# Experts 2 to 8 in the order of their load, with rooms cut to rank and a folded last tile

## The chip, the cores and the metric

The kernel runs on one core of one Trainium2 chip. The metric is the device time in microseconds (us) from one launch: the median over the runs that are shown. Engines are named as the profile names them: PE (TensorE, matrix products), PEld (its weight loads), DVE (VectorE), ACT (ScalarE), POOL (GpSimd) and SP (SyncE, which here only starts transfers).

## The reference

Attention of 4 batches, 8 heads, 576 positions and 64 per head, once over means of four positions and once over a band of |i - j| < 4, is added up to rows `x` (2304 x 512). Each row then goes to the 2 of 8 experts with the highest noisy gate value:

```python
logits = x @ w_gate
noisy_logits = logits + np.log1p(np.exp(x @ w_noise)) * noise
top2 = np.argpartition(-noisy_logits, 2, axis=1)[:, :2]
# top2_w: softmax over the two values
for e in range(E):
    for k in range(2):
        mask = top2[:, k] == e
        h = np.maximum(x[mask] @ w1[e], 0.0)            # 512 x 1024
        out[mask] += top2_w[mask, k, None] * (h @ w2[e])  # 1024 x 512
```

Everything is float32. For the reference's own inputs the eight experts get 619, 579, 568, 539, 545, 556, 609 and 593 rows.

## The kernel before

**Number format.** Products of the experts run in the type fp32r, each operand split in a high part (the operand rounded by a copy to fp32r) and a low part (what is left). A product is three: high x high, low x high, high x low.

**Early part (up to 232 us).** Attention, gating, the lists of rows per expert, and all of expert 0. Its work is written as steps (`Step`), each with an engine, a planned duration, buffers and a priority. `run_steps` plans: of the steps that can run it takes the one that starts first, priority breaking ties, and emits the instructions in that order. The priority is that of the step's place plus an offset by kind from the table `OFF` (L322). Stages 1 to 3 of this plan follow one another. For each row the two list entries (row number and weight) are scattered into `list_d` in DRAM (`r_put`); expert e's list begins at `e * LST`. After the last group of rows `c_count` adds up the counts and `c_tiles` works out how many tiles of 128 rows stand beyond each expert's room, `CAP` = 630 slots.

**Experts 1 to 7.** This part is written out in program order, in a loop over the experts. `NT` = 5 tiles of `TR` = 126 rows are an expert's room; 632 columns in two halves of 316 are multiplied. For expert e:

- `gemm1(e, f)`, f = 0 to 7: PE multiplies 128 columns of w1 (the weights in the array) with the 2 x 316 columns of `xh`, `xl` (2 halves x 4 chunks x 3 products = 24 products). ACT takes the relu out of PSUM into `hh`, DVE the rest into `hl`. PSUM has two buffers for this.
- `gemm2(e, t)`, t = 0 to 4: 126 rows of `hh`, `hl` are the weights in the array and w2 streams 512 columns (8 chunks x 3 products = 24). DVE scales by the row's weight and adds what stands in `out` (fetched by `load_acc`); POOL scatters the sum to `out`.

Beside these, by the table `BESIDE` (slots 0 to 7 are the groups of `gemm1`, 8 to 12 the tiles of `gemm2`), the next expert's rows are brought: `gather` (G, POOL), `turn_xt` (T, a 32 x 32 transpose on DVE), `move_xt` (M, N; copies of 32 partitions, half on ACT, half on DVE) and `make_xt` (H, the split in high and low). The order of tile 4 is G4 in slot 9, T4 in 10, M4 and N4 in 11, H4 in 12. SP fetches w2 in the course of `gemm1` and the next expert's w1 in the course of `gemm2`, through three buffers `raw`; ACT and DVE split them (`split_hi`, `split_lo`). At the start of an expert SP loads the next one's list (`load_list`) and DVE limits its row numbers (`list_rows`).

**Beyond the room.** At the end all engines read whether any expert has more rows than its room; if so, a block loads that expert's weights (w1 and w2, 4.19 MB) anew and works through further tiles of 128 rows with nothing beside it.

Of the kernel before, what the change touches and what calls it, by code (L numbers as in the profile page):

```python
# [22 lines left out]
def kernel(  # L23
# [12 lines left out]
    nc = tc.nc  # L36
# [33 lines left out]
    LST = P * ((CAP + P * ((N - CAP + P - 1) // P) + P - 1) // P)  # L70
    FAR = 4096
    PST = 4
# [39 lines left out]
    counts = cpool.tile([P, E], F32, tag="counts", name="counts")  # L112
    cnt16 = cpool.tile([P, E], BF16, tag="cnt16", name="cnt16")
# [20 lines left out]
    def c_route():  # L134
# [9 lines left out]
                       allow_small_or_imprecise_dtypes=True)  # L144
        nc.gpsimd.iota(base_e, pattern=[[LST, E]], base=0, channel_multiplier=0,
# [40 lines left out]
    raws = {}  # L186

    def fetch_w(e, z, f):
        if z == 0:
            raw = stage.tile([P, NDC, P], F32, tag="raw", name="raw1")  # L190
            nc.sync.dma_start(out=raw, in_=w1[e, :, f * P : (f + 1) * P].rearrange("(c p) f -> p c f", p=P))
# [82 lines left out]
    def run_steps(stage):  # L274
# [48 lines left out]
        "a_acc": -44.2, "a_count": -60, "a_holes": 6, "a_list": 10.6, "a_part": -60, "a_rows": 25.3,  # L323
        "b_gather": -60, "b_gemm": 30.3, "b_hi": 10.9, "b_list": -11.9, "b_lo": -21.5, "b_order": -10.6,
        "b_pe": -23.8, "b_relu": -27.6, "b_rest": -44.4, "b_rows": 35.1, "b_weights": -26.1, "c_count": -49,
        "c_fills": 39, "c_first": -42.1, "c_ids": -17.6, "c_masks": -48.5, "c_route": -37.4, "c_sel": -58.3,
        "c_tiles": -59, "d_exp": -3.6, "d_max": -23.4, "d_norm": 16.4, "d_pt": -8.8, "d_ptc": -15.8,
        "d_pv": -48.8, "d_qk": -27.5, "d_rz": 44.4, "d_up": -8.5, "e_go": 43.4, "e_hi": -60, "e_lo": 46.5,
        "e_order": -58.5, "e_pe": -2.9, "fetch_e": 11.3, "fetch_w1": 31.8, "fetch_w2": 20.9,
        "fill_list": -37.6, "fill_out": 41.4, "gather": 18.4, "hi_e": 51.9, "identb": 30, "init_kz": 60,  # L330
        "l_exp": -60, "l_lg": -27.3, "l_lgc": 27.8, "l_lgt": -15.1, "l_load_v": 26.2, "l_ls": -19.8,
        "l_max": 23.1, "l_norm": -10.7, "l_pt": 7.2, "l_ptc": 21.8, "l_pv": 10.8, "l_qk": 1.7,
        "l_store": -24.5, "l_sum": 50.9, "l_x": -58.2, "l_xt": -20.9, "l_xtc": 26.7, "list_rows": 3.3,
        "lo_e": -50.5, "load_list": 59.2, "load_noise": 30.4, "load_wgn": -14.6, "masks": 17, "o_mul": -60,
        "o_part": -15, "o_put": 41.7, "ones": 2.2, "r_count": 52.3, "r_hot": -5.6, "r_oh": -20.5, "r_pay": -29,
        "r_pos": -35.2, "r_put": 17.7, "r_slot": 37, "r_soft": -59.5, "r_top": -52.3, "r_wexp": 53.9,
        "r_where": -60, "split_hi1": 28.3, "split_hi2": -26.7, "split_lo1": 60, "split_lo2": 29.4,
        "t_copy": -52.9, "t_load": -18, "t_new": 16.1, "t_pe": 11.6, "t_sum": 14.9, "t_sumq": -28.2,
        "vd_load": -1.6, "vd_sum": 2.8, "vd_sum2": 26.4, "warm": 30.2}
# [759 lines left out]
    def load_list(e):  # L1099

        src = list_d[e * LST : e * LST + NT * P, :]
        lt = l_p.tile([P, NT, 2], I32, tag="lt", name=f"lt{e}")
        wait_for(nc.sync.dma_start(out=lt, in_=src.rearrange("(p t) c -> p t c", t=NT)), scatters)
        lists[e] = lt, None

    def list_rows(e):
        lt = lists[e][0]
        cl = l_p.tile([P, NT], I32, tag="cl", name=f"cl{e}")
        nc.vector.tensor_scalar_min(cl, lt[:, :, 0], N - 1)
        lists[e] = lt, cl  # L1110
# [9 lines left out]
    def gather(e, t):  # L1120
        gx = gx_p.tile([P, DM], F32, tag="gx", name=f"gx{e}_{t}")
        ins = nc.gpsimd.indirect_dma_start(  # L1122
            out=gx, out_offset=None, in_=x_rows[:, :],
            in_offset=bass.IndirectOffsetOnAxis(ap=lists[e][1][:, t : t + 1], axis=0))
# [3 lines left out]
    def new_xt(e):  # L1128
        xeT[e] = (xe_p[e % 2].tile([P, NDC, NCOL], F32R, tag="xh", name=f"xh{e}"),
                  xe_p[e % 2].tile([P, NDC, NCOL], F32R, tag="xl", name=f"xl{e}"))  # L1130
# [58 lines left out]

# [3 lines left out]

    def c_tiles():
        nc.vector.tensor_copy(cnt_f[:, 0:E], st.pop("pc"))
        nc.vector.tensor_tensor(cnt_f[:, 0:1], cnt_f[:, 0:1], base_e[:, 0:1], op=ALU.add)
        nc.vector.tensor_reduce(out=cnt_f[:, E:], in_=cnt_f[:, 0:E], axis=AX.X, op=ALU.max)
        nc.vector.tensor_scalar(cnt_f, cnt_f, float(P - 1 - CAP), 0.0, op0=ALU.add, op1=ALU.max)
# [5 lines left out]
    def turn_xt(e, t):  # L1204
        tr = gx_p.tile([P, 4, NDC, 32], F32, tag="tr", name=f"tr{e}_{t}", bufs=2)
        nc.vector.transpose(out=tr, in_=gxs.pop((e, t)).rearrange("p (a c j) -> p a c j", a=4, c=NDC))
        trs[e, t] = tr

    def move_xt(e, t, us):
# [3 lines left out]
        for u in us:  # L1213
            for a in range(4):
# [5 lines left out]

    def make_xt(e, t):
# [3 lines left out]
        sl = slice(t * TR, t * TR + P)  # L1225
        xr = xrs.pop((e, t)).rearrange("p u (c i) -> p c u i", c=NDC)
        xh, xl = (x_[:, :, sl].rearrange("p c (u i) -> p c u i", u=4) for x_ in xeT[e])
# [6 lines left out]
    def o_part(t, c):  # L1234
# [4 lines left out]
        for f in range(OC * c, OC * (c + 1)):  # L1239
            hh, hl = hts[f]  # L1240
# [21 lines left out]
    def e_hi(t):  # L1262
        if t == 0:
            new_xt(1)
        sl, src = cols(t)
        nc.scalar.activation(xeT[1][0][:, :, sl], st["ptg", t][:, :, src], AF.Copy)

    def e_lo(t):
        sl, src = cols(t)
        nc.vector.tensor_tensor(xeT[1][1][:, :, sl], st.pop(("ptg", t))[:, :, src], xeT[1][0][:, :, sl].bitcast(F32), op=ALU.subtract)  # L1270
# [5 lines left out]

    def gemm1(e, f):
        xh, xl = xeT[e]
        wh, wl = w1s[f]
        ph = ps_h.tile([P, 2, 512], F32, tag="sc", name=f"ph{e}_{f}")  # L1280
        for n in range(2):
            sl = slice(n * NH, (n + 1) * NH)
# [4 lines left out]
        hts[f] = (h_p.tile([P, NCOL], F32R, tag=f"hh{f}", name=f"hh{e}_{f}"), h_p.tile([P, NCOL], F32R, tag=f"hl{f}", name=f"hl{e}_{f}"))  # L1287
        hh, hl = (x.rearrange("p (n m) -> p n m", n=2) for x in hts[f])
        nc.scalar.activation(hh, ph[:, :, 0:NH], AF.Relu)  # L1289
        nc.vector.scalar_tensor_tensor(out=hl, in0=ph[:, :, 0:NH], scalar=0.0, in1=hh.bitcast(F32),  # L1290
# [226 lines left out]
```

## Time and profile before

| | |
|---|---|
| median of 3 runs | 633.02 us (632.44 to 633.78) |
| the profiled execution: its time | 634.73 us |
| its span, first to last instruction | 633.0 us |
| mean granted TensorE clock in the span | 0.981 of full |
| busy: PE, PEld, DVE, ACT, POOL | 603.8, 525.9, 398.7, 335.6, 239.7 us |
| moved between HBM and core | 72.62 MB read, 19.95 MB written |

The span is measured inside one profiled execution; its time has what lies around the span as well. A busy share is a mean over parts of the kernel with different limits. PE's matmuls overlap and their ends are modelled, so the pace of a run of products is read from the chain, as its length over their number, and not from the duration of one.

### The profile page before, as it was taken

What the parts mean: (1) busy time and instruction counts of PE and PEld (TensorE: products, weight loads), DVE (VectorE), ACT (ScalarE), POOL (GpSimd) and SP (SyncE); (2) the same over time, 40 slices, a digit from 0 to 9 for tenths busy, and PEclk for the clock granted to TensorE, in tenths of its full rate; (3) what the DMA queues carried; (4) which work ended last, traced back from release to release, by engine and by line L of the source; (5) the groups of instructions that cost most, each with busy time, mean ns of one, the idle gap of its engine ahead of it and who ended that gap; (6) DMA issues with size and microseconds to landing.
All of it is one profiled execution on the core that took longest, in us unless ns stands there. A gap on an engine that the chain in (4) does not pass through costs nothing.

```text
span 633.0 us, 12482 instructions
## 1 busy us (share of the span) xinstructions
PE 603.8 (95%) x4598; PEld 525.9 (83%) x4598; DVE 398.7 (63%) x1019; ACT 335.6 (53%) x770; POOL 239.7 (38%) x310
## 2 busy tenths in 40 slices
PE   8899997998998999999999999999999999999993
PEld 7668775767987889889988988998899899889982
DVE  5987797896865445873775587377458737754310
ACT  7967785775644224752763475266357526633200
POOL 6585457762564423323222322323232232322111
PEclk9999999898899999999999999999999999999997
DMA  9987888967545715444553545455354545444111
GB/s 193 164 169 150 210 197 165 252 189 204 155 112 140 222 44 170 132 145 152 150 154 112 165 124 152 142 153 155 116 155 129 160 143 143 150 131 123 52 47 35
DMA packets 137010, 92.61 MB, mean 146 GB/s; under 512 B 72280, under 2 KB 118872, under 8 KB 136940
## 3 DMA queue, kind: packets, MB, share of 16 engines
q1 hardware_dynamic: 125388, 62.71, 40.4%
q0 software_dynamic: 11552, 29.01, 15.0%
q8 instruction: 38, 0.62, 0.4%
q14 instruction: 32, 0.26, 0.2%
HBM read 72.62 MB, written 19.95 MB: 146 GB/s over the span
## 4 chain that ended last, share of the span: by engine, by line
PE 82%; DMA 7%; ACT 3%; POOL 3%; DVE 2%; issue 1%; SPq 1%; POOLq 0%; DVEq 0%
PE ph L1285 31%; PE py L1310 31%; PE py L1243 3%; PE o L661 3%; DMA raw<-in_moe_w_dram 2%; PE ph0b L1170 2%; PE sc L613 2%; PE pt L438 2%; DMA vw<-in_v_dram 2%; PE ptx L692 1%; PE od L576 1%; PE ptl L646 1%; DMA vg<-in_v_dram 1%; POOL list_d L869 1%; PE ptd L554 1%
## 5 line engine op out<-in xcount | busy, mean ns | idle before, releaser
L1285 PE MATMUL ph<-xl,w0h 128*128 128x316 f32 x448 | 137.9, 308 | 0.0
L1285 PE MATMUL ph<-xh,w0l 128*128 128x316 f32 x448 | 137.8, 308 | 0.0
L1285 PE MATMUL ph<-xh,w0h 128*128 128x316 f32 x448 | 137.7, 307 | 0.0
L1289 ACT ACTIVATE hh<-ph 128x632 fp32r<-128x632 f32 x56 | 39.2, 700 | 134.8 <-PE ph L1285 134.8
L1310 PE MATMUL py<-w1h,hl 128*126 128x512 f32 x280 | 110.4, 394 | 0.0
L1310 PE MATMUL py<-w1h,hh 128*126 128x512 f32 x280 | 110.3, 394 | 0.0
L1310 PE MATMUL py<-w1l,hh 128*126 128x512 f32 x280 | 110.3, 394 | 0.0
L1290 DVE SCALAR_TENSOR_TENSOR hl<-ph,hh 128x632 fp32r<-128x632 f32 x56 | 45.7, 817 | 85.0 <-ACT hh L1289 85.0
L1316 POOL DMA_INDIRECT out_dram<-ga,lt x35 | 39.2, 1120 | 155.0 <-DVE ga L1315 123.7
L1285 PEld LDWEIGHTS ph<-xh,w0h 128*128 128x128 f32 x448 | 84.3, 188 | 0.3
L1285 PEld LDWEIGHTS ph<-xl,w0h 128*128 128x128 f32 x448 | 84.3, 188 | 0.3
L1285 PEld LDWEIGHTS ph<-xh,w0l 128*128 128x128 f32 x448 | 84.2, 188 | 0.0
L1217 ACT ACTIVATE xr<-tr 32x128 f32<-32x128 f32 x240 | 74.0, 308 | 3.4
L1315 DVE SCALAR_TENSOR_TENSOR ga<-py,lt,ga 126x512 f32<-126x512 f32 x35 | 26.3, 751 | 68.2 <-PE py L1310 68.2
L1298 POOL DMA_INDIRECT ga<-out_dram,cl x35 | 37.6, 1073 | 82.8 <-PE ph L1285 61.0
L201 ACT ACTIVATE w0h<-raw 128x512 fp32r<-128x512 f32 x64 | 39.4, 625 | 48.4 <-DMA raw<-in_moe_w_dram 48.2
L1310 PEld LDWEIGHTS py<-w1l,hh 128*126 128x126 f32 x280 | 52.1, 186 | 12.9
L1310 PEld LDWEIGHTS py<-w1h,hh 128*126 128x126 f32 x280 | 52.2, 186 | 12.6
L1310 PEld LDWEIGHTS py<-w1h,hl 128*126 128x126 f32 x280 | 52.1, 186 | 12.5
L1219 DVE COPY xr<-tr 32x128 f32<-32x128 f32 x240 | 54.6, 227 | 3.0
L1122 POOL DMA_INDIRECT gx<-x_d,cl x35 | 36.7, 1048 | 51.9 <-PE ph L1285 33.4
L869 POOL DMA_INDIRECT list_d<-pay,sli x36 | 36.9, 1025 | 43.1 <-DMA x_d<-x 12.8
(196 smaller groups left out, 1080.5 us busy)
## 6 DMA issues: line engine op xcount, KB each, us to landing
raw<-in_moe_w_dram SPq DMA_DIRECT2D x128, 256.0 KB
vw<-in_v_dram SPq DMA_DIRECT2D x80, 64.0 KB
x_d<-x SPq DMA_DIRECT2D x18, 256.0 KB
out_dram<-zero SPq DMA_DIRECT2D x6, 768.0 KB
nat<-in_q_dram SPq DMA_DIRECT2D x16, 256.0 KB
nat<-in_k_dram SPq DMA_DIRECT2D x16, 256.0 KB
vg<-in_v_dram SPq DMA_DIRECT2D x8, 320.0 KB
vg<-in_v_dram SPq DMA_DIRECT2D x8, 256.0 KB
```

The costliest lines, as they stand in the source:

```text
L201: nc.scalar.activation(hi, raw, AF.Copy)
L869: ins = nc.gpsimd.indirect_dma_start(out=list_d[:, :], out_offset=bass.IndirectOffsetOnAxis(ap=sli[:, kk, i : i + 1], axis=0), in_=pay[:, ...
L1122: ins = nc.gpsimd.indirect_dma_start(out=gx, out_offset=None, in_=x_rows[:, :], in_offset=bass.IndirectOffsetOnAxis(ap=lists[e][1][:, t : ...
L1217: nc.scalar.activation(dst, src, AF.Copy)
L1219: nc.vector.tensor_copy(dst, src)
L1285: last_mm[0] = nc.tensor.matmul(ph[:, n, 0:NH], lhsT=w[:, c, :], rhs=xx[:, c, sl], start=(c == 0 and z == 0), stop=(c == NDC - 1 and z == 2))
L1289: nc.scalar.activation(hh, ph[:, :, 0:NH], AF.Relu)
L1290: nc.vector.scalar_tensor_tensor(out=hl, in0=ph[:, :, 0:NH], scalar=0.0, in1=hh.bitcast(F32), op0=ALU.max, op1=ALU.subtract)
L1298: after_pe(nc.gpsimd.indirect_dma_start(out=acc[:TR], out_offset=None, in_=out[:, :], in_offset=bass.IndirectOffsetOnAxis(ap=cl[:TR, t : t ...
L1310: last_mm[0] = nc.tensor.matmul(py[:TR], lhsT=hx[:, sl], rhs=w, start=(f == 0 and z == 0), stop=(f == NFC - 1 and z == 2))
L1315: nc.vector.scalar_tensor_tensor(out=acc[:TR], in0=py[:TR], scalar=wt, in1=acc[:TR], op0=ALU.mult, op1=ALU.add)
L1316: nc.gpsimd.indirect_dma_start(out=out[:, :], out_offset=bass.IndirectOffsetOnAxis(ap=lt[:TR, t, 0:1], axis=0), in_=acc[:TR], in_offset=No ...
```

## The change

The seven experts after expert 0 are taken in the order of their number of rows, largest first. The order is worked out on the chip (`c_rank`) and a register on SP holds each rank's expert number (`read_which`); weights and lists are fetched at addresses from that register. Rank r has a room of its own: 512 slots in four tiles of 128 rows, and a last tile of 112, 96, 80 and four times 64 slots, that is 624, 608, 592 and 4 x 576. Expert 0 stays first, with its room of 630 in tiles of 126.

`gemm1` multiplies two halves of 312, 304, 296 or 288 columns. Where the last tile has 64 slots, the columns of `x` are placed so that each half has two tiles and 32 of the tail; the relu and its rest are taken out in two pieces, and `h` is laid out so that the tail's high and low parts stand side by side. `gemm2` of this tile loads them as 128 rows against the high part of w2 (rows 0 to 63 then have high x high, rows 64 to 127 low x high) and adds high x low to rows 0 to 63: 16 products for 24. The lower rows are then copied out of PSUM by ACT and added by DVE ahead of the scaling.

Lists are loaded in two pieces; gathers, transposes and splits of the last tile work on its rows alone. In the early part there are two more steps (`c_rank` on DVE, `which` on SP), and `load_list` and `fetch_e` of expert 1 wait for the latter. Every number of the table `OFF` is another. `LST` grows from 2432 to 2560 slots.

```diff
-    LST = P * ((CAP + P * ((N - CAP + P - 1) // P) + P - 1) // P)
+    LST = P + P * ((CAP + P * ((N - CAP + P - 1) // P) + P - 1) // P)
+    MAIN = (NT - 1) * P
+    FOLD = 64
+    HALF = 2 * P + FOLD // 2
+    TAIL = [None, 112, 96, 80] + [FOLD] * (E - 4)
+    def cap(r):
+        return MAIN + TAIL[r] if r else CAP
...
+    def read_which(r):
+        which[r] = nc.values_load(perm[0:1, r : r + 1], engines=[mybir.EngineType.SP], min_val=0, max_val=E - 1,
...
-            nc.sync.dma_start(out=raw, in_=w2[e, f * P : (f + 1) * P, :])
+            nc.sync.dma_start(out=raw, in_=w2[at(e), f * P : (f + 1) * P, :].rearrange("o p m -> p (o m)"))
...
-        "b_gather": -60, "b_gemm": 30.3, "b_hi": 10.9, "b_list": -11.9, "b_lo": -21.5, "b_order": -10.6,
...
+        "b_gather": -3.4, "b_gemm": 25.5, "b_hi": 52.1, "b_list": 24.7, "b_lo": -51.8, "b_order": 10.4,
...
+        n = got(e, NT - 1)
+        for dst, s0, rows in (lt[:, : NT - 1], 0, MAIN), (lt[:n, NT - 1 :], MAIN, n):
+            src = list_d[bass.ds(which[e] * LST + s0, rows), :]
+            wait_for(nc.sync.dma_start(out=dst, in_=src.rearrange("(p t) c -> p t c", t=dst.shape[1])), scatters)
...
+    def c_rank():
...
+        nc.vector.tensor_copy(cnt, st.pop("pc"))
+        nc.vector.scalar_tensor_tensor(out=key, in0=cnt, scalar=float(E), in1=iota_e, op0=ALU.mult, op1=ALU.subtract)
+        nc.vector.memset(key[:, 0:1], float(1 << 20))
+        nc.vector.tensor_tensor(prod, along(key), across(key), op=ALU.is_gt)
+        nc.vector.tensor_reduce(out=rank, in_=prod, axis=AX.X, op=ALU.add)
+        nc.vector.tensor_tensor(hot8, along(rank), across(iota_e), op=ALU.is_equal)
+        nc.vector.tensor_tensor(prod, hot8, along(iota_e), op=ALU.mult)
+        nc.vector.tensor_reduce(out=perm_f, in_=prod, axis=AX.X, op=ALU.add)
+        nc.vector.tensor_copy(perm, perm_f)
...
+    def place(e, t, x_):
+        if TAIL[e] > FOLD:
+            return x_[:, :, t * P : t * P + got(e, t)].rearrange("p c (u i) -> p c u i", i=32)
+        if t < NT - 1:
+            s0 = t // 2 * HALF + t % 2 * P
+            return x_[:, :, s0 : s0 + P].rearrange("p c (u i) -> p c u i", i=32)
+        return x_[:, :, : 2 * HALF].rearrange("p c (n m) -> p c n m", n=2)[:, :, :, 2 * P :]
...
     def gemm1(e, f):
+        nh = cap(e) // 2
...
-                    last_mm[0] = nc.tensor.matmul(ph[:, n, 0:NH], lhsT=w[:, c, :], rhs=xx[:, c, sl],
+                    last_mm[0] = nc.tensor.matmul(ph[:, n, 0:nh], lhsT=w[:, c, :], rhs=xx[:, c, sl],
...
+        for (hh, hl), src in ((main, ph[:, :, 0 : nh if TAIL[e] > FOLD else 2 * P]), (tail, ph[:, :, 2 * P : nh])):
+            if hh is None:
+                continue
+            hh, hl = (x_.rearrange("p (n m) -> p n m", n=2) for x_ in (hh, hl))
+            nc.scalar.activation(hh, src, AF.Relu)
+            nc.vector.scalar_tensor_tensor(out=hl, in0=src, scalar=0.0, in1=hh.bitcast(F32), op0=ALU.max, op1=ALU.subtract)
...
     def gemm2(e, t):
+        m = tok(e, t)
+        folded = m == FOLD
...
+            if folded:
+                both = hts[f][:, s0 : s0 + 2 * FOLD]
+                terms = ((both, wh, 2 * FOLD), (both[:, :FOLD], wl, FOLD))[:: -1 if f else 1]
...
+        if folded:
+            low = gx_p.tile([P, DM], F32, tag="tr", name=f"low{e}", bufs=2)
+            nc.scalar.activation(low[:m], py[FOLD : 2 * FOLD], AF.Copy)
+            nc.vector.tensor_tensor(low[:m], low[:m], py[:m], op=ALU.add)
+            src = low[:m]
...
-    Step("c_tiles", "dve", 1.1, c_tiles, after=[a1], use=[pb], prio=42, stage=3)
+    s_rank = Step("c_rank", "dve", 1.9, c_rank, after=[a1], use=[pb], prio=30, stage=3)
+    Step("c_tiles", "dve", 1.5, c_tiles, after=[s_rank], prio=42, stage=3)
+    s_which = Step("which", "sp", 0.5, lambda: read_which(1), after=[s_rank], prio=30, stage=3)
...
+            read_which(e + 1)
             load_list(e + 1)
```

## Rows read from the trace of the kernel before

**Rows 1.** The page's engine line: busy us, share of the span, instructions.
```profile
PE 603.8 (95%) x4598; PEld 525.9 (83%) x4598; DVE 398.7 (63%) x1019; ACT 335.6 (53%) x770; POOL 239.7 (38%) x310
```

**Rows 2.** The chain that ended last: start us, length us, engine, tile, line.
```profile
232.02 27.84 PE ph L1285 x192
259.86 27.86 PE py L1310 x120
287.72 27.97 PE ph L1285 x192
...
622.32 0.76 DVE ga L1315
```

**Rows 3.** Windows up to 206 us: busy us (instructions), granted clock, DMA share, GB/s.
```profile
95.00:110.80 15.80, 11.81 (x163) 9.23 (x161) 12.19 (x47) 9.04 (x19) 12.54 (x20) 0.90 0.85 165
110.80:126.60 15.80, 15.18 (x194) 12.14 (x194) 13.95 (x30) 11.51 (x22) 12.24 (x19) 0.88 0.97 252
...
142.40:158.30 15.90, 13.46 (x229) 11.21 (x227) 9.97 (x51) 7.99 (x15) 4.03 (x5) 0.82 0.75 204
...
sum 206.00, PE 187.52 PEld 152.60 DVE 159.25 ACT 139.26 POOL 121.96; mean PE 14.42 PEld 11.74 DVE 12.25 ACT 10.71 POOL 9.38
```

**Rows 4.** The same chain, expert 0's second half of the first product.
```profile
198.65 11.60 PE ph0b L1170 x96
```

**Rows 5.** Windows inside L1170's 256 columns, L1285 and L1310: PE busy, then PEld.
```profile
199.00:209.00 10.00, 10.00 (x86) 10.00 (x86) 5.29 (x11) 4.35 (x10) 3.36 (x4) 1.00 0.46 120
235.00:255.00 20.00, 20.00 (x140) 20.00 (x139) 11.40 (x22) 10.67 (x23) 6.97 (x7) 1.00 0.50 153
262.00:285.00 23.00, 23.00 (x100) 18.44 (x99) 17.13 (x43) 13.61 (x34) 6.17 (x5) 1.00 0.44 135
```

**Rows 6.** Groups by line and shape: busy us, mean ns, idle us before.
```profile
L1285 PEld LDWEIGHTS ph<-xh,w0h 128*128 128x128 f32 x448 | 84.3, 188 | 0.3
...
L1310 PEld LDWEIGHTS py<-w1h,hh 128*126 128x126 f32 x280 | 52.2, 186 | 12.6
...
L452 ACT ACTIVATE kz<-pt 64x512 f32<-64x512 f32 x32 | 18.7, 590 | 1.9 <-PE pt L438 1.5
...
L1184 DVE SCALAR_TENSOR_TENSOR hl<-ph0b,hh 128x254 fp32r<-128x254 f32 x8 | 3.4, 420 | 2.5 <-ACT hh L1180 2.5
...
L1180 ACT ACTIVATE hh<-ph0b 128x254 fp32r<-128x254 f32 x8 | 3.0, 377 | 4.2 <-PE ph0b L1170 4.2
...
L846 DVE TENSOR_REDUCE slf<-oh 128x8 f32<-128x64 f32 x4 | 0.9, 220 | 0.1
```

**Rows 7.** Timeline of expert 3's seventh group (f = 6) on ACT and DVE; [idle before].
```profile
365.84 1.28 ACT L1217 ACTIVATE xr<-tr 32x128 f32<-32x128 f32 x4
...
367.14 0.63 ACT L1228 ACTIVATE xh<-xr 128x512 fp32r<-128x512 f32 x1
...
367.94 0.70 ACT L1289 ACTIVATE hh<-ph 128x632 fp32r<-128x632 f32 x1 [0.17 <-PE ph L1285]
...
368.67 0.82 DVE L1290 SCALAR_TENSOR_TENSOR hl<-ph,hh 128x632 fp32r<-128x632 f32 x1 [0.18 <-ACT hh L1289]
```

**Rows 8.** Timeline where expert 2 ends and expert 3 begins.
```profile
339.88 0.68 DVE L1229 TENSOR_TENSOR xl<-xr,xh 128x512 fp32r<-128x512 f32 x1
...
343.38 0.30 PE L1285 MATMUL ph<-xh,w0h 128*128 128x316 f32 x1
```

**Rows 9.** Line L1446, a register load: duration ns min/median/max, start us.
```profile
L1446 SPq TENSOR_LOAD <-cnt_i x1: 486/486/486, 184.1 to 184.1; - x1
L1446 SPq FUSED_REGOPS  x1: 183/183/183, 184.7 to 184.7; - x1
```

**Rows 10.** The chain that ended last, behind the count of the rows.
```profile
190.92 5.80 DMA raw<-in_moe_w_dram
...
196.75 0.64 ACT w1h L201
```

**Rows 11.** Line L1316, the scatter to `out`.
```profile
DMA to landing us min/median/max: 3.0/4.2/4.4
```

More of the change, by code (lines that the diff above doesn't have):

```diff
@@ L112 @@
     counts = cpool.tile([P, E], F32, tag="counts", name="counts")
+    cap_e = cpool.tile([P, E], F32, tag="cap_e", name="cap_e")
     cnt16 = cpool.tile([P, E], BF16, tag="cnt16", name="cnt16")
@@ L144, in c_route @@
                        allow_small_or_imprecise_dtypes=True)
+        for r in range(E):
+            nc.gpsimd.memset(cap_e[:, r : r + 1], float(P - 1 - cap(r)))
         nc.gpsimd.iota(base_e, pattern=[[LST, E]], base=0, channel_multiplier=0,
@@ L186, with at @@
     raws = {}
+    which = {}
+    def at(r):
+        return bass.ds(which[r], 1) if r else slice(0, 1)
+    def read_which(r):
+        which[r] = nc.values_load(perm[0:1, r : r + 1], engines=[mybir.EngineType.SP], min_val=0, max_val=E - 1,
+                                  skip_runtime_bounds_check_because="a sum over a one-hot of the numbers 0 to E - 1")
     def fetch_w(e, z, f):
@@ L328 @@
[L328 to L337, printed above, removed]
@@ L1224, in make_xt @@
             new_xt(e)
-        sl = slice(t * TR, t * TR + P)
-        xr = xrs.pop((e, t)).rearrange("p u (c i) -> p c u i", c=NDC)
-        xh, xl = (x_[:, :, sl].rearrange("p c (u i) -> p c u i", u=4) for x_ in xeT[e])
+        nu = got(e, t) // 32
+        xr = xrs.pop((e, t))[:, :nu].rearrange("p u (c i) -> p c u i", c=NDC)
+        xh, xl = (place(e, t, x_) for x_ in xeT[e])
         nc.scalar.activation(xh, xr, AF.Copy)
@@ L1275, with h_cols @@
     hts = [None] * NFC
+    def h_cols(e, h):
+        if not e or TAIL[e] > FOLD:
+            w = cap(e) if e else NCOL
+            return (h[:, :w], h[:, NCOL : NCOL + w]), (None, None)
+        return (h[:, :MAIN], h[:, MAIN + 2 * FOLD : 2 * MAIN + 2 * FOLD]), (h[:, MAIN : MAIN + FOLD], h[:, MAIN + FOLD : MAIN + 2 * FOLD])
     def gemm1(e, f):
@@ L1304, in gemm2 @@
         py = ps_t.tile([P, DM], F32, tag="tp", name=f"py{e}_{t}")
-        sl = slice(t * TR, (t + 1) * TR)
+        m = tok(e, t)
+        folded = m == FOLD
+        s0 = t * P
         for f in range(NFC):
-            hh, hl = hts[f]
+            (hh, hl), _ = h_cols(e, hts[f])
             wh, wl = w2s[f]
-            for z, (hx, w) in enumerate(((hh, wh), (hl, wh), (hh, wl))):
-                last_mm[0] = nc.tensor.matmul(py[:TR], lhsT=hx[:, sl], rhs=w, start=(f == 0 and z == 0),
-                                 stop=(f == NFC - 1 and z == 2))
+            if folded:
+                both = hts[f][:, s0 : s0 + 2 * FOLD]
+                terms = ((both, wh, 2 * FOLD), (both[:, :FOLD], wl, FOLD))[:: -1 if f else 1]
+            else:
+                terms = tuple((hx[:, s0 : s0 + m], w, m) for hx, w in ((hh, wh), (hl, wh), (hh, wl)))
+            for z, (hx, w, rows) in enumerate(terms):
+                last_mm[0] = nc.tensor.matmul(py[:rows], lhsT=hx, rhs=w, start=(f == 0 and z == 0),
+                                 stop=(f == NFC - 1 and z == len(terms) - 1))
         lt = lists[e][0]
-        wt = lt[:TR, t, 1:2].bitcast(F32)
+        wt = lt[:m, t, 1:2].bitcast(F32)
         acc = accs.pop((e, t))
-        nc.vector.scalar_tensor_tensor(out=acc[:TR], in0=py[:TR], scalar=wt, in1=acc[:TR], op0=ALU.mult, op1=ALU.add)
+        src = py[:m]
+        if folded:
[3 more added lines that the diff above has]
+            src = low[:m]
+        nc.vector.scalar_tensor_tensor(out=acc[:m], in0=src, scalar=wt, in1=acc[:m], op0=ALU.mult, op1=ALU.add)
         nc.gpsimd.indirect_dma_start(
-            out=out[:, :], out_offset=bass.IndirectOffsetOnAxis(ap=lt[:TR, t, 0:1], axis=0),
-            in_=acc[:TR], in_offset=None, bounds_check=N - 1, oob_is_err=False)
+            out=out[:, :], out_offset=bass.IndirectOffsetOnAxis(ap=lt[:m, t, 0:1], axis=0),
+            in_=acc[:m], in_offset=None, bounds_check=N - 1, oob_is_err=False)
     R.update({"ph": Ring(3, True), "xr": Ring(2)})
@@ L1364 @@
         Step("o_put", "pool", 1.25, lambda t=t: o_put(t), after=[a1_], use=[gab], prio=60 + 5 * t, lag=3.0, stage=3)
-    a1 = Step("load_list", "sp", 0.9, lambda: load_list(1), after=list(s_put), prio=33, move=0.3, stage=3)
+    a1 = Step("load_list", "sp", 0.9, lambda: load_list(1), after=list(s_put) + [s_which], prio=33, move=0.3, stage=3)
     a1 = Step("list_rows", "dve", 1.0, lambda: list_rows(1), after=[a1], prio=33, stage=3)
@@ L1376 @@
         rb = buf("raw")
-        a1 = Step("fetch_e", "sp", 0.45, lambda f=f: fetch_w(1, 0, f), new=[rb], prio=70 + f, move=1.2, stage=3)
+        a1 = Step("fetch_e", "sp", 0.45, lambda f=f: fetch_w(1, 0, f), after=[s_which], new=[rb], prio=70 + f, move=1.2, stage=3)
         a2 = Step("hi_e", "act", 0.52, lambda f=f: w1_again(f, True), after=[a1, s_g[f]], use=[rb], prio=70 + f, stage=3)
```

112 lines of the change are left out of this document (71 added, 41 removed).

## Prediction

> **What bounds the kernel now.** I read the page's engine line first [rows 1]: PE is busy 95% of the span, the next engine 63%. A modelled busy share doesn't prove that PE sets the end, so the chain that ended last comes next [rows 2]. The reader is to see there that from 232.02 us to 622.3 us, when the last scaling on DVE starts, the chain has pieces of PE alone: for each of experts 1 to 7 one of 192 products (`gemm1`, L1285), then one of 120 (`gemm2`, L1310). Nothing else stands between them, so in these 390 us time is number of products times pace. The first product takes 27.84 us, in three of the seven 27.97, so 27.90 on average or 145.3 ns each (316 columns); the second 27.86 us, 232.2 ns each (512 columns). Behind the last product come one scaling on DVE and the scatter on POOL.
>
> Ahead of 232 us it is otherwise. In the windows up to 206 us PE is busy 187.5 us [rows 3]: 18.5 us are idle, the worst slice has 4.0 us of it, and in one slice the granted clock is 0.82, so 36% of it ran at 1.2 GHz instead of 2.4. There the order of the steps matters, and the change deals that order anew through OFF.
>
> **The change part by part.**
>
> *Narrower first product.* Half the room replaces 316: 312, 304, 296 and four times 288 columns. That takes 4 + 12 + 20 + 4 x 28 = 148 columns off, times 192 products: 28,416 columns. What is a column worth? Expert 0's second half streams 256 columns with weights of the same shape: 96 products in 11.60 us, 120.8 ns each [rows 4]. From 256 to 316 columns that is 24.5 ns for 60, 0.408 ns per column; from 316 to 512 it is 86.9 for 196, 0.443. The new widths lie between 256 and 316, so I take 0.408: **-11.6 us**; the other end is -12.6.
>
> One row looks as if it spoke against this: in the first product PE's weight loads are busy all of the time, 20.00 of 20 us, and in the second 18.44 of 23 [rows 5]. But at 256 columns they are busy all of the time too (10.00 of 10), and there the same loads of 188 ns [rows 6] came every 120.8 ns. They overlap, so their busy time is no floor at 145 ns, nor at the 133.9 ns that I expect of 288 columns. The Trainium skill, Perfetto Trace Analysis, section "Identifying the Most-Contended Engine", says that TensorE's distance from its bound is to be judged by the busy share of LDWEIGHTS and not by that of the matmuls; by it the first product would be bound by loads, which the change leaves at 192 of 128 columns, and that term would be 0. The 256-column row disagrees.
>
> *Folded last tile.* For the four smallest experts the last tile takes 16 products instead of 24, since [high | low] goes against the high weights at once as 128 rows: 4 x 8 x 232.2 ns = **-7.4 us**. The first four tiles become 128 rows wide instead of 126. No row has 512 columns of this type with 128 rows; the load rows differ by 2 ns (188 against 186 [rows 6]), which on the 4 x 24 x 7 = 672 products would be +1.3 us if it came on the path. I take nothing, because a row with 128-wide loads kept a pace of 120.8; the end is kept.
>
> *Tail at the end.* The last expert is folded, so between its last product and its scaling stand an ACT copy of 64 x 512 out of PSUM (0.590 us by the copy of that shape [rows 6]) and a DVE add (0.68 by a 128x512 operation [rows 8]), with two hand-overs of some 0.03 us: **+1.3 us**. Nothing hides it. In the three other folded experts the same work lies under the next expert's product.
>
> *Two evictions for one.* A folded expert's f has main (512) and tail (64) columns. For 254 columns ACT took 377 ns and DVE 420 [rows 6], for 632 columns 700 and 820 [rows 7]; on the line between, 0.60 and 0.69 for 512, and at its foot 0.2 and 0.22 for the tail (estimates from those rows): +0.1 us each. What hides it: PE has two `ph` buffers, so f's pair must end within one product group after its own, 24 x 133.9 ns = 3.21 us. The fullest group on ACT also carries four moves (1.28), one `xh` (0.63) and one weight copy (0.62 to 0.63): 0.8 + 1.28 + 0.63 + 0.63 = 3.34 us, a little over 3.21, and before it was idle just 0.17 us there [rows 7]. That group is late by 0.1 to 0.3 us, the next (without `xh`) takes 2.7 and makes it good. `hl` ended at 368.67 + 0.82, 1.6 us after its products released ACT at 367.94, so 1.6 us of cover are left: 0. Without that cover it is 0.1 us a group.
>
> *Boundaries.* The tail's columns now stand in both halves, so the next expert's first product wants `xh`/`xl` of tile 4 at once and not 1.7 us later. Before, tile 4's `xl` ended at 340.56, 2.8 us before that product at 343.38 [rows 8]. A folded last tile lasts 3.72 us instead of 5.57, so the margin falls to 0.9, and the work on 64 rows for 128 gives some back. 0; see the rivals.
>
> *Ranking.* `c_rank` is nine DVE operations of 128 x 8 to 128 x 64, up to 0.22 us each by the reduce of 128 x 64 [rows 6], 2.0 us; `c_tiles` has two more, 0.4. `which` is a register load on SP: 0.49 + 0.18 us by the one that SP does today [rows 9]. In the chain at that place DVE frees `raw` buffers for the fetches of w2 and PE waits behind them: a fetch runs 5.80 us from 190.92 and only then is the next part of w2 ready [rows 10]. So 2.4 us on DVE could all pass to PE, 3.1 with the register load, or nothing. With the plan unknown I take **+0.5**, nearer to nothing: the piece that the chain waits for at 190.92 is the fetch itself, more than twice as long as the ranking. In SP's queue the fetches of w1 and the list wait behind `which`; the first product of expert 1 is 40 us off.
>
> *Per expert* SP gets another such load (0.7 us), two list loads for one, and 16 fetches with an address from a register. No row shows such a fetch; between nothing and one register load each, 0 to 11 us of SP per expert of 52, hidden since PE waits for no fetch after 232 us [rows 2]. Smaller gathers and scatters take POOL work off: nothing.
>
> *New order of the steps up to 232 us.* Below: all 18.5 us of idleness can't be won. Above: one more stretch like the worst slice is +4.0. Both signs are open, so 0, with 4.5 either way.
>
> Sum: -11.6 - 7.4 + 1.3 + 0.5 = **-17.2 us**. The profiled execution had a span of 633.0 and a time of 634.73, so it would have 615.8 and 617.5; its 634.73 stands 1.7 above the median of 633.02, from which the forecast is **615.8 us**. The known terms alone leave 614.3 to 620.0 (-12.6 and no ranking cost; +1.3 for wider loads, +3.1 for the ranking, tail 1.6).
>
> **Rivals.**
> 1. *The new order gives a better early stage* by over 4.5 us: below 611. For: idleness and low clock are there [rows 3]. Against: it also has to place more steps. 0.09.
> 2. *It gives a worse one* by over 4.5 us: 620.5 to 628. The same rows, and one more step in front of w2's splits [rows 10]. 0.11.
> 3. *The first product is bound by weight loads*, as the rule above has it: -7.4 + 1.8, 627.4 us. Against: 120.8 ns with the same loads [rows 4]. 0.03.
> 4. *Folded boundaries stall.* Three times a folded tile stands ahead of a product. If `xl` of tile 4 ends over 0.9 us later in its tile than now (a late fetch of w1 is enough, since ACT's weight copies stand in front of `xh`), each costs about 1 us: 619. 0.04.
> 5. *Slower: an expert does not fit its room.* Then the overflow block loads 4.19 MB of weights with nothing beside it: at the best slice's 252 GB/s [rows 3] 16.6 us, to which gather, 40 products that nothing hides and scatter come (a scatter's landing alone is 3.0 to 4.4 us [rows 11]): over +20 for one tile, about 637 us. It decides from one token too many. Against: for the reference's inputs I count 609, 593, 579, 568, 556, 545 and 539 in experts 1 to 7 by load, against rooms of 624, 608, 592, 576; the nearest has 8 spare. 0.02.
>
> The rest, 0.71, is the forecast, with 611 to 620.5 as its own range.
>
> **How the numbers follow.** 611 to 620.5 holds 0.71 and rival 4's 0.04. Half a microsecond on each side takes in a part of rivals 1 and 2, so the range is **610.5 to 621**, about 8 in 10. A measurement here tells about 0.2% (1.3 us) from no change. Slower is rival 5 and a thin end of rival 2 (it would take 17 us more in the early stage): 0.03. Same: 0.01. Faster: 0.96.
>
> **What would show it.** In the chain of the changed kernel: the first products at about 27.6, 27.0, 26.3 and four times 25.7 us, the second at 27.86 three times and 26.0 four times, nothing between them; behind the last product an ACT copy and two DVE operations. The start of expert 1's first product near 232.5 us: any distance from it is the order's doing. Wrong it would be if the chain named a weight load, ACT or DVE at a boundary, if 288 columns kept 145 ns, or if the early stage had moved by over 5 us.

## The result and the profile after

The changed kernel took **623.97 us** (median of 4 runs, 622.84 to 624.76) against 633.4 of before in the same comparison (632.44 to 635.54): a ratio of 0.9845, 95% interval 0.9814 to 0.9876. That is faster, as forecast, but by 1.2 to 1.9% where 2.7% was forecast; the time is 8.2 us above the forecast of 615.8 and 3 us above its range. The profiled execution has a span of 623.0 us and a time of 624.76.

The engine line of the page after, which answers to [rows 1]:

```profile
PE 585.3 (94%) x4555; PEld 503.9 (81%) x4555; DVE 402.8 (65%) x1053; ACT 332.7 (53%) x786; POOL 237.7 (38%) x318
```

PE has 18.5 us less to do, but the span fell by only 10.0. The chain that ended last says where (start us, length us, what; dots stand for lines left out; it answers to [rows 2]):

```profile
239.62 27.55 PE ph L1366 x192
267.17 27.95 PE py L1402 x120
295.11 26.66 PE ph L1366 x192
...
349.74 26.20 PE ph L1366 x192
...
403.85 22.27 PE ph L1366 x168
426.12 0.06 issue
426.18 3.42 PE ph L1366 x24
429.60 26.42 PE py L1402 x112
...
585.60 25.94 PE py L1402 x112
611.54 0.02 issue
611.56 0.60 ACT low L1410
...
612.18 0.69 DVE low L1411
...
612.90 0.76 DVE ga L1413
```

From expert 1's first product to the end of the last one it is 371.9 us for 390.3: **-18.4**. Behind it are the copy and the addition, and the span ends 0.8 us later after its last product than before. But expert 1's first product starts at 239.62 and not at 232.02: **+7.6**. The sum, -10.0, is the whole difference of the spans. The loss of 7.6 us stands ahead of the experts.

What is lost there? One row of the windows up to that product, for the kernel before and then for the changed one (sum of the stretch, busy us of each engine):

```profile
sum 232.00, PE 213.52 PEld 174.57 DVE 171.25 ACT 145.85 POOL 130.11; mean PE 71.17 PEld 58.19 DVE 57.08 ACT 48.62 POOL 43.37
```

```profile
sum 239.60, PE 213.53 PEld 174.20 DVE 173.67 ACT 144.99 POOL 131.18; mean PE 71.18 PEld 58.07 DVE 57.89 ACT 48.33 POOL 43.73
```

PE is busy just as long. All 7.6 us are waiting. The chain of this stretch names transfers: first in the changed kernel, then in that of before, from a scatter into the lists (`list_d<-pay,sli`) over the load of a list (`lte`) to the fetches of weights (`raw`):

```profile
172.21 6.06 DMA list_d<-pay,sli
...
178.39 0.39 SPq L1059
...
178.84 2.17 DMA lte<-list_d
...
186.03 5.16 DMA gx<-x_d,cl
...
193.47 7.50 DMA raw<-in_moe_w_dram
...
202.37 7.83 DMA raw<-in_moe_w_dram
```

```profile
170.10 3.84 DMA list_d<-pay,sli
...
174.07 0.39 SPq L1031
...
174.52 3.19 DMA lte<-list_d
...
185.04 4.47 DMA raw<-in_moe_w_dram
```

The scatter starts 2.1 us later than before and takes 2.2 us longer to land, so the list is asked for 4.3 us later; its load is 1.0 us shorter, so it is there 3.3 us later (181.01 for 177.71). Behind it a gather of rows of `x` (5.16 us) and two fetches of weights (7.50 and 7.83 us) hold the chain, where before two fetches held it for 4.47 and 5.80 [rows 10]: from the list to the end of the second fetch it is 29.2 us for 19.0. Of these 10.2 us the stretch from there to expert 1 gives back 5.9 (29.4 us for 35.3). The view of DMA issues has the scatters of the whole run, 36 in each kernel, with the median us from issue to landing (the signal that the transfer is done): first before, then after.

```profile
list_d<-pay,sli POOLq DMA_INDIRECT x36, 5.1
```

```profile
list_d<-pay,sli POOLq DMA_INDIRECT x36, 6.0
```

The median is over the scatters whose landing the trace shows, 4 of the 36 before and 10 after, so by itself it says little.

### The profile page after: what moved, and what is told of

Same layout as the page of the kernel before. It is cut to its first block, busy times and chain, and to the rows that moved or that the text cites. A ratio compares the mean times of both kernels' runs of the same rounds, so it can differ in the third digit from the quotient of the medians.

```text
span 623.0 us, 12762 instructions
## 1 busy us (share of the span) xinstructions
PE 585.3 (94%) x4555; PEld 503.9 (81%) x4555; DVE 402.8 (65%) x1053; ACT 332.7 (53%) x786; POOL 237.7 (38%) x318
## 3 DMA queue, kind: packets, MB, share of 16 engines
q1 hardware_dynamic: 126076, 62.72, 41.8%
## 4 chain that ended last, share of the span: by engine, by line
PE 68%; DVE 9%; DMA 8%; ACT 5%; issue 4%; POOL 4%; SPq 1%; POOLq 0%; DVEq 0%; ACTq 0%
PE py L1402 30%; PE ph L1366 29%; PE py L1317 4%; DMA raw<-in_moe_w_dram 3%; ACT kz L480 2%; DMA vw<-in_v_dram 2%; POOL list_d L897 1%; DMA vg<-in_v_dram 1%; DMA list_d<-pay,sli 1%; ACT pd L564 1%; DVE pd L575 1%; DVE sb L653 1%; DMA gx<-x_d,cl 1%; DVE xT L711 1%; DVE mx L651 1%
## 5 line engine op out<-in xcount | busy, mean ns | idle before, releaser
L1402 PE MATMUL py<-w1h,h 128*128 128x512 f32 (+3 forms) x528 | 168.1, 395 | 0.0
L1366 PE MATMUL ph<-xh,w0h 128*128 128x288 f32 (+3 forms) x448 | 133.5, 298 | 0.1
L1366 PE MATMUL ph<-xh,w0l 128*128 128x288 f32 (+3 forms) x448 | 133.5, 298 | 0.0
L1366 PE MATMUL ph<-xl,w0h 128*128 128x288 f32 (+3 forms) x448 | 133.5, 298 | 0.0
L1402 PEld LDWEIGHTS py<-w1h,h 128*128 128x128 f32 (+3 forms) x528 | 97.3, 185 | 26.3 <-ACT w1h L229 1.2
L1402 PE MATMUL py<-w1l,h 128*128 128x512 f32 (+4 forms) x280 | 110.1, 395 | 0.0
L1376 DVE SCALAR_TENSOR_TENSOR h<-ph,h 128x512 fp32r<-128x512 f32 (+3 forms) x88 | 48.1, 546 | 62.8 <-ACT h L1375 62.6
L1383 POOL DMA_INDIRECT ga<-out_dram,cl x35 | 35.9, 1024 | 72.4 <-PE ph L1366 53.2
L1402 PEld LDWEIGHTS py<-w1l,h 128*128 128x128 f32 (+4 forms) x280 | 50.3, 179 | 14.3 <-DVE w1l L234 1.3
L234 DVE TENSOR_TENSOR w1l<-raw,w1h 128x512 fp32r<-128x512 f32 x64 | 44.0, 687 | 18.3 <-ACT w1h L229 18.2
L234 DVE TENSOR_TENSOR w0l<-raw,w0h 128x512 fp32r<-128x512 f32 x64 | 43.4, 705 | 9.7 <-ACT w0h L229 9.6
```

What stands on the lines that cost most here:

```text
L234: nc.vector.tensor_tensor(lo, raws.pop((e, z, f)), hi.bitcast(F32), op=ALU.subtract)
L1366: last_mm[0] = nc.tensor.matmul(ph[:, n, 0:nh], lhsT=w[:, c, :], rhs=xx[:, c, sl], start=(c == 0 and z == 0), stop=(c == NDC - 1 and z == 2))
L1376: nc.vector.scalar_tensor_tensor(out=hl, in0=src, scalar=0.0, in1=hh.bitcast(F32), op0=ALU.max, op1=ALU.subtract)
L1383: after_pe(nc.gpsimd.indirect_dma_start(out=acc[: tok(e, t)], out_offset=None, in_=out[:, :], in_offset=bass.IndirectOffsetOnAxis(ap=cl[: ...
L1402: last_mm[0] = nc.tensor.matmul(py[:rows], lhsT=hx, rhs=w, start=(f == 0 and z == 0), stop=(f == NFC - 1 and z == len(terms) - 1))
```

## The experiments

Each ratio is to the kernel before in the same comparison, with its 95% interval. There were three comparisons, in which before had medians of 634.9 (the first four kernels), 634.28 (*a_lst2432*, *b_lst2560*, *a_static*, *a_lst_evict*) and 637.13 us (the other four), so times are set against each other within one comparison, and across them by ratio only. A start of expert 1 is read from one profiled execution of each kernel, and it too is set against others of the same comparison.

**Theory 1: the new table.** The chain shows transfers in another order; by theory 1 it is the new `OFF` that costs the 7.6 us, by its narrower forms the offset of one kind of step, `fetch_e` or `fill_out`. Its rivals have other places in the diff: the added steps, and what else changed in the early part.

*a_oldoff*: the changed kernel with the table of before. (`l_pv` and `r_pos` have the same number in both tables, and the two new kinds of step keep their new ones.)

```diff
-        "a_acc": -36.4, "a_count": -2.3, "a_holes": 2.5, "a_list": 42.7, "a_part": -8.5, "a_rows": -0.9,
+        "a_acc": -44.2, "a_count": -60, "a_holes": 6, "a_list": 10.6, "a_part": -60, "a_rows": 25.3,
...
+        "vd_load": -1.6, "vd_sum": 2.8, "vd_sum2": 26.4, "warm": 30.2, "c_rank": -60, "which": 56.2}
```

> The changed kernel with the table OFF of the kernel before (its two new kinds c_rank and which keep their new offsets). Measured so far: expert 1's first product starts at 239.62 us in the changed kernel against 232.02 before, 7.6 us later, while the part behind it is 18.4 us shorter. Theory 1, the new table costs the 7.6 us: the product starts at 232 to 233.5 us and the time is 616 to 618 us. Theory 2, the added steps (ranking on DVE, register load on SP) cost it: the start stays at 238 to 240 us and the time at 623 to 625 us.

Measured: 625.13 us, 0.9843 (0.9782 to 0.9904), not to be told from the new table's 0.9845. Expert 1 starts at 240.12.

*b_newoff*: the kernel before with the new table, the same edit the other way.

> The kernel before with the new table OFF and nothing else of the change. Theory 1 (the table): its first product of expert 1 starts at 238 to 240 us, the time is 639 to 641 us, slower than before by 6 to 8 us. Theory 2 (the added steps): start at 232 us, 633 us.

Measured: 638.54 us, 1.0043 (1.0012 to 1.0075). The new table costs the old kernel some 2.7 us (0.0043 x 634.9), not 7.6, and in the changed kernel no cost of it is seen. Its scatters land in 4.6 us, no later than before; expert 1 starts between what the two theories forecast:

```profile
236.82 27.84 PE ph L1285 x192
```

*a_fetch_e* and *a_fill_old*: one offset each, in the changed kernel.

```diff
-        ... "fetch_e": -15.1, ...
+        ... "fetch_e": 11.3, ...
```

> The changed kernel with one number of its table set back: fetch_e from -15.1 to the old 11.3. In the changed kernel's order SP issues fetches of expert 1's w1 between the last fetches of expert 0's w2 (six of w2, then w1, w2, w1, w2, then w1); here all eight of w2 come first, the order ahead of them is the same. Theory 1a, these w1 fetches hold the three raw buffers until expert 0 is done with its own w1, so that w2 and the second product of expert 0 come late: the start of expert 1 falls by 4.5 to 6 us to 234 to 235 us, time 618 to 620 us. Theory 1b, the loss lies ahead in the attention part (loads of v behind the fill of out): no more than 1 us, 623 to 624 us.

```diff
-        ... "fill_out": 56.7, ...
+        ... "fill_out": 41.4, ...
```

> The changed kernel with one other number set back: fill_out from 56.7 to the old 41.4, which spreads the transfers that zero out among other loads instead of putting three in a row ahead of two loads of v (PE waits there 4.4 and 1.9 us for v). Theory 1b: the start of expert 1 falls by 4 to 7 us, time 617 to 620 us. Theory 1a: the wait ahead is given back later, since w2 sets the end of the early part: less than 2 us, 622 to 624 us.

Measured: 626.65 us, 0.9876 (0.9838 to 0.9913), and 629.11 us, 0.9927 (0.9894 to 0.9960). Neither brings anything back: both are above what 1a and 1b forecast, with expert 1 at 241.88 and 244.63 us, and the second makes the kernel slower. In the three of these runs that keep the new `LST`, the scatters land in 5.8, 5.8 and 6.8 us. Theory 1 fell with its narrower forms.

**Theory 3: the distance between the lists.** What is left are the added steps (ranking, register loads), which is theory 2, and, as theory 3, the one line of the diff that the prediction never priced: `LST`, 2560 slots for 2432, which sets the bytes from one expert's list to the next, 20,480 for 19,456 (a slot has 8). So the old `LST` in the changed kernel, the new one in the kernel before, and the changed kernel without the ranking:

*a_lst2432* (*b_lst2560* is the same edit in the kernel before, the other way):

```diff
-    LST = P + P * ((CAP + P * ((N - CAP + P - 1) // P) + P - 1) // P)
+    LST = P * ((CAP + P * ((N - CAP + P - 1) // P) + P - 1) // P)
```

> The changed kernel with the old stride of the lists, LST 2432 in place of 2560, and nothing else. Seen so far: from 176 to 212 us a scatter into the lists lands after a median of 3.8 and 3.2 us in the two kernels with stride 2432 and after 5.9 to 6.8 us in the four with 2560, and everything of expert 0 waits for scatters there. Theory 3, the stride of 2560 slots (20480 bytes) slows the scatters, and with them the early part: landings of 3 to 4 us, expert 1's first product starts 4 to 7 us earlier, at 233 to 236 us, time 617 to 620 us. Theory 2, the ranking steps are it: landings may fall, but the start stays within 2 us of 239.6, 622 to 624 us.

> The kernel before with LST 2560 and nothing else of the change. Theory 3 (stride): landings of 5.5 to 7 us from 176 to 212 us, start of expert 1's first product at 235 to 238 us, 3 to 6 us slower than before. Theory 2 (ranking): no difference beyond 0.3%.

*a_static*:

```diff
+    ORDER = [0, 6, 7, 1, 2, 5, 4, 3]
+    which = dict(enumerate(ORDER))
...
-        return bass.ds(which[r], 1) if r else slice(0, 1)
+        return slice(which[r], which[r] + 1)
...
-    s_rank = Step("c_rank", "dve", 1.9, c_rank, after=[a1], use=[pb], prio=30, stage=3)
...
-    s_which = Step("which", "sp", 0.5, lambda: read_which(1), after=[s_rank], prio=30, stage=3)
```

> The changed kernel with the order of the experts written in as constants (1, then 7, 8, 2, 3, 6, 5, 4, which is their order for these inputs): the ranking steps, the register loads and the waits for them are left out, rooms, folding, stride 2560 and table stay. Theory 2 (the added steps cost the early part): start at 232 to 235 us, time 616 to 619 us. Theory 3 (stride): start at 237 to 239.5 us, 0 to 2.5 us faster than the changed kernel, the estimate of the ranking in the prediction being 0.5.

Measured: *a_lst2432* 616.96 us, 0.9731 (0.9682 to 0.9779). *b_lst2560* 642.17 us, 1.0108 (1.0057 to 1.0159). *a_static* 628.39 us, 0.9896 (0.9844 to 0.9947).

One line moves both kernels by about the same amount: 0.0108 x 634.28 = 6.9 us up in the kernel before (3.6 to 10.1 by the interval, 3 to 6 forecast), (0.9845 - 0.9731) x 634.28 = 7.2 us down in the changed one (some 3.5 to 11, since two comparisons are set side by side). Taking the ranking out gains nothing, so it can't be what is lost; *a_static* even starts expert 1 later than either theory forecast, and why is not known (its plan has fewer steps and so another order). In the chains, first the changed kernel with the old distance, then the kernel before with the new one, then *a_static*:

```profile
232.15 27.55 PE ph L1366 x192
```

```profile
174.40 7.15 DMA list_d<-pay,sli
...
239.89 27.84 PE ph L1285 x192
```

```profile
242.94 27.51 PE ph L1336 x192
```

Expert 1 starts at 232.15 with 2432 in the changed kernel and at 239.89 with 2560 in the old kernel, where the scatter in the chain takes 7.15 us; in the trace of before, from the first comparison, it was 232.02 and 3.84. The views of DMA issues of these three and of *a_lst_evict* have no landing times for the 36 scatters.

In each of the comparisons that have both, every kernel with 2432 starts expert 1 ahead of every one with 2560: 232.02 against 239.62 in the first pair; 236.82 (*b_newoff*) against 240.12, 241.88 and 244.63; 232.15 and 233.48 (*a_lst_evict*) against 239.89 and 242.94.

**Size or address?** 2560 differs from 2432 in two ways: the lists are longer (more to fill at the start), and 20,480 bytes is 5 x 4096, while 19,456 is 4.75 x 4096. By 3a it is the addresses, by 3b the size. Two longer lists tell them apart, the first by being longer without being a multiple: 2688 slots are 21,504 bytes, 5.25 x 4096; 3072 are 24,576 bytes, 6 x 4096.

*a_lst2688* and *a_lst3072*:

```diff
+    LST = 2688
```

> The changed kernel with LST 2688, a list area larger still (21504 bytes per expert, 1024 x 21; 2560 slots are 20480 bytes, 4096 x 5; 2432 are 19456, 1024 x 19). Theory 3a, the addresses matter: with a stride that is a multiple of 4096 bytes the places that the eight lists have come to fall together in the memory behind them, with another they don't; then this one is as fast as 2432: start of expert 1 at 232 to 234 us, time 616 to 618 us. Theory 3b, the size of the lists matters (they are filled with padding first): slower than with 2560, 624 to 627 us.

```diff
+    LST = 3072
```

> The changed kernel with LST 3072, 24576 bytes per expert, 8192 x 3. Theory 3a: at least as slow as 2560, 624 to 632 us. Theory 3b, by size: 20% more padding than 2560, 624 to 630 us too; only together with the run at 2688 does it tell them apart. If it is as fast as 2432 (617 us), neither holds and 20480 bytes are special for another reason.

Measured: *a_lst2688* 621.2 us, 0.9752 (0.9710 to 0.9794), by its ratio not to be told from 2432 (0.9731) though the lists are longer than with 2560. Its time and its start (238.01) lie above the forecast, 616 to 618 and 232 to 234, but so do the starts of the kernels with 2432 in this comparison: *a_nofold*, further down, has the same early part and starts expert 1 at 238.93. *a_lst3072* 661.64 us, **1.0411** (1.0367 to 1.0455), is 40 us slower than 2688, far beyond both forecasts. The chain of 2688 and the DMA views, first of 2688, then of 3072 (packets, MB, share of 16 engines' span; the scatters' landing):

```profile
238.01 27.55 PE ph L1366 x192
```

```profile
q1 hardware_dynamic: 126076, 62.73, 41.5%
...
list_d<-pay,sli POOLq DMA_INDIRECT x36, 4.8
```

```profile
q1 hardware_dynamic: 126076, 62.75, 44.5%
...
list_d<-pay,sli POOLq DMA_INDIRECT x36, 13.1
```

The scatters, the same 36 of 128 slots, land in 4.8 and in 13.1 us (medians of the 13 and 8 landings that the traces show). Other transfers pay too: the same 126,076 packets of queue 1 take 0.445 x 656.0 = 291.9 us of all 16 engines for 0.415 x 621.2 = 257.8. In the chain of 3072 the fetches of weights hold longer, and expert 1 starts 34.6 us later than in *a_lst2688*:

```profile
193.28 10.15 DMA raw<-in_moe_w_dram
...
219.89 10.84 DMA raw<-in_moe_w_dram
...
272.62 2.44 PE ph L1366 x17
```

So 3b falls, and 3a fits all four distances tried: slow at 5 and 6 times 4096 bytes, fast at 4.75 and 5.25 times. The four don't fix the rule itself: the fast ones are odd multiples of 1024 bytes, so slow at every multiple of 2048 would fit as well. Nor is it shown where the lists lie in DRAM; whether another `LST` also moves their beginning is open.

**The folded tile.** *a_nofold* has the old distance and takes the last tile's products as 24 again, with one eviction for each group.

```diff
-    FOLD = 64
+    FOLD = 32
...
-    TAIL = [None, 112, 96, 80] + [FOLD] * (E - 4)
+    TAIL = [None, 112, 96, 80] + [64] * (E - 4)
```

> Stride 2432, and the last tile of 64 rows not folded: 24 products in place of 16, eviction in one piece, no low rows to add; rooms and widths stay. By the prediction's terms it is 7.4 - 1.3 = 6.1 us slower than a_lst2432; with the three waits of 0.45 us that came with the two-piece eviction taken off, 4.8 us: 621.5 to 623.5 us, the second products of the small experts 27.9 us each. Rival: folding gains nothing since the wait for the low rows goes round: 617 us.

Measured: 626.14 us, 0.9840 (0.9803 to 0.9877), against 0.9731 with the fold: 0.0109 x 634.28 = 6.9 us, with some 4 either way, and more than the 4.8 forecast. The two runs are of different comparisons, and their early parts, which are the same program, differ by 6.8 us in the traces (238.93 for 232.15), so the fold is better read behind them. The chain of *a_nofold* at experts 1, 4 and 7, then the last product of *a_lst2432*:

```profile
238.93 27.55 PE ph L1366 x192
...
403.16 25.44 PE ph L1366 x192
428.60 27.98 PE py L1402 x120
...
588.98 28.02 PE py L1402 x120
```

```profile
577.90 25.94 PE py L1402 x112
```

From expert 1's first product to the end of the last one it is 378.1 us without the fold and 371.7 with it (232.15 to 603.84). Less the 1.3 us that the copy and the addition take at the end, the fold is worth **5.0 us**, near the 4.8 forecast. The rival, that folding gains nothing, is out.

**The two-piece eviction.** In the changed kernel three of the folded experts' second products take 26.42 and not 25.94 us. The timeline after shows why (start us, us; in brackets the idle time before and its releaser):

```profile
483.74 0.60 ACT L1375 ACTIVATE h<-ph 128x512 fp32r<-128x512 f32 x1
...
484.76 0.65 DVE L1376 SCALAR_TENSOR_TENSOR h<-ph,h 128x512 fp32r<-128x512 f32 x1
...
485.45 0.22 ACT L1375 ACTIVATE h<-ph 128x64 fp32r<-128x64 f32 x1 [1.11 <-DVE h L1376]
485.69 0.63 ACT L229 ACTIVATE w1h<-raw 128x512 fp32r<-128x512 f32 x1
...
486.38 0.30 PEld L1402 LDWEIGHTS py<-w1h,h 128*128 128x128 f32 x2 [0.43 <-ACT w1h L229]
```

ACT's second copy (`h` is one tile now, for both pieces) waits 1.11 us for DVE's subtraction of the first piece. The last copy of w2 stands behind it on ACT, and PE's next weight load waits 0.43 us for that copy; by the chain the whole second product loses 0.48 us. *a_lst_evict* has the old distance and takes both ACT copies first:

```diff
+        rests = []
...
             nc.scalar.activation(hh, src, AF.Relu)
+            rests.append((hh, hl, src))
+        for hh, hl, src in rests:
```

> Stride 2432 as in a_lst2432, and in gemm1 of the folded experts both copies of ACT are issued ahead of both operations of DVE, not in the order ACT, DVE, ACT, DVE. In the changed kernel ACT's 64-column copy waits 0.76 to 1.11 us for DVE's main piece, and in three of the four folded experts PE then waits about 0.45 us for the last part of w2. If the two engines only take turns because of the order of issue, the second products of these experts take 26.0 us in place of 26.42 and the time is 1.3 us below that of a_lst2432; if the turn is forced by the tile (one tile holds all four pieces), nothing changes.

Measured: **616.04 us**, 0.9704 (0.9659 to 0.9748), the lowest of all. The chain has lost the stalls, in the first product too:

```profile
397.71 25.44 PE ph L1366 x192
423.15 25.90 PE py L1405 x112
449.05 25.48 PE ph L1366 x192
474.53 25.92 PE py L1405 x112
```

By the chains, beside *a_lst2432*, this is worth 1.6 us in the second products and 0.4 in the first; the medians differ by 0.9 us, which the intervals don't tell from nothing.

**The table once more**, with the old distance and the new eviction. *a_old_lst_evict* has these two edits and the table of *a_oldoff*.

> The table OFF of the kernel before, stride 2432 and ACT's copies ahead of DVE's operations; beside a_lst_evict it tells what the new table is worth when the stride is not in the way. With the kernel before and stride 2432 the new table cost 3.6 us; if that holds here, the start of expert 1 falls from 233.5 to 230 us and the time to 612 to 613 us; if the new table suits the added steps, 617 to 620 us.

Measured: 621.42 us, 0.9776 (0.9737 to 0.9814), against 0.9704 with the new table. The new table looks better here by some 4.6 us, but the intervals overlap a little and the comparisons differ; the start of expert 1, 237.59, is no later than that of the other kernels with an old or near distance in its comparison (238.01, 238.93), which have the new table. With 2560 the two tables could not be told apart; whether the slow scatters covered a real gain isn't settled.

## Why the prediction was wrong

**The missed step** is one that isn't in the sum: `LST`. The document ahead of the prediction names it, and the prediction has no term, bound or rival for it. Under "new order of the steps up to 232 us" the early part had 0 with 4.5 either way, so the sum was right about the place of the risk but wrong about its cause and size: +7.6 us in the trace, 6.9 and 7.2 us by the two runs that changed this line alone. The prediction's own sign of being wrong, an early stage that moves by over 5 us, came; but its reading of that sign, that any distance of expert 1's start from 232.5 us is the order's doing, failed as well. Rival 2, "it gives a worse one", has the right interval (620.5 to 628) for the wrong reason: the old table gives 0.9843, the new 0.9845. The trace of before could have warned only in part. It shows that the list loads wait for the scatters, but no trace of it has another distance. With +7.2 the sum would have been 615.8 + 7.2 = 623.0.

**Without that line the sum holds.** The changed kernel with 2432 took 616.96 us; by ratio on the median from which the forecast started, 0.9731 x 633.02 = 616.0 (612.9 to 619.0), against 615.8. That it comes so near is in part luck: the terms below are off by up to 1.4 us each, and the errors cancel.

- *Narrower first product*: -11.6 forecast, -12.4 measured (182.9 for 195.3 us in all seven), inside the two ends. Two of the seven hold stalls of the two-piece eviction; without them, in *a_lst_evict*, it is 182.3 us and -13.0, past the far end of -12.6. 288 columns take 25.48 / 192 = 132.7 ns, not 133.9, so a column is worth 0.45 ns and not 0.408.
- *Weight loads as a bound* (rival 3): out. The loads still take 188 ns each and the pace fell from 145.3 to 132.7 ns. The rule of the Trainium skill that was weighed there (Perfetto Trace Analysis, "Identifying the Most-Contended Engine"), as the prediction applied it, would have left this product at 27.9 us. The page names two measures, MFU (the share of peak arithmetic) and the busy share of LDWEIGHTS, and does not say that busy loads bind; the prediction took the second alone and read that into it.
- *Folded tile*: -7.4 forecast, -6.0 measured (189.0 for 195.0 us). The three unfolded experts give back 0.25 us, since 128 rows take 27.91 to 27.96 us and not 27.86. The folded ones take 26.42 three times and 25.94 once, where 26.0 was forecast; in *a_lst_evict* they take 25.90 to 25.94, and the term is -7.5.
- *Two evictions*: forecast 0 behind 1.6 us of cover. The durations were right: 0.597 and 0.225 us on ACT, 0.683 and 0.225 on DVE. What was missed is the order, ACT-DVE-ACT-DVE on one tile, in which ACT alone waits 1.11 us for 0.22 us of work; it cost 0.48 us in the second product of three experts and 0.3 in the first product of two.
- *Tail at the end*: +1.3 forecast, and the chain has 1.34 us from 611.56 to 612.90.
- *Boundaries* (rival 4): no wait at any of them; each product starts where the one before it ends.
- *Ranking*: +0.5 forecast, no cost seen. *a_static* is not faster than the changed kernel (0.9896 against 0.9845). *SP's loads*: 0, as forecast; no fetch is in the chain behind 239.62.
- *Overflow* (rival 5): it did not come. *A better early stage* (rival 1): it got longer.

**What stays open**: what in the memory slows the scatters. The runs show the dependence on the distance, at 20,480 bytes in both kernels and at four distances in the changed one, and nothing below it. All eight lists are filled at once, so that entries of one scatter for different experts lie about a whole number of distances apart; that such addresses fall on the same part of the memory when the distance is a multiple of 4096 bytes is an argument and no measurement. Nor is it known why at 20,480 bytes only the scatters from 140 us on are slower. The two loads that hold the chain longer were seen, but not which of their packets were slow.

## What to carry to other kernels

Price every constant of a diff that sets addresses, also one that seems to change only a size: 128 slots of padding took back 7 of the 17 us that the rest gained, and 128 more gave most of them back. When one stage is late and its busy time is unchanged, compare the landing time of each transfer before looking at the order of the steps. When one eviction becomes two, issue both operations of the first engine before those of the second, since each turn between two engines on one tile can be a wait (1.11 us here) that what stands behind it inherits.

## What the runs showed of the hardware

Scatters of 128 slots of 8 bytes over eight lists land, by the distance of the lists, in 4.6 to 5.1 us at 19,456 bytes (medians of four kernels), 4.8 at 21,504, 5.8 to 6.8 at 20,480 (four kernels) and 13.1 at 24,576; the last slows the whole kernel by 4.1% against before. The traces show the landing of 4 to 19 of the 36 scatters of a kernel. Taken together by distance, those that start from 140 us on land after a median of 4.6 us at 19,456 bytes (27 landings), 4.7 at 21,504 (7), 6.1 at 20,480 (34) and 11.2 at 24,576 (4); those ahead of 140 us after 6.3 (21), 5.0 (6), 5.8 (25) and 15.0 (4). As far as these landings tell, 20,480 bytes slow the later scatters alone, 24,576 both.

The Trainium skill has a relative of this in DMA: Bandwidth & Descriptors, section "Latency and other measured facts": copies whose rows in HBM lie large powers of two apart, 512 KiB and more, lose bandwidth, and 4 KiB more between the rows restores it, with aliasing of memory channels as an inference. The runs here agree in kind, that a distance alone can slow a transfer, but at 20 and 24 KiB and for single slots; and the added bytes that cured it here were 1 KiB (20,480 to 21,504), while another 4 KiB (20,480 to 24,576) made it worse.
